# Other start addresses for TensorE's operands: moving ones at 160, stationary ones at 384 bytes modulo 512

## The chip, the cores and the metric

The kernel runs on one core of one Trainium2 chip. The metric is the device time of one execution in microseconds (us). On-chip memory (SBUF) has 128 partitions, and a tile takes the same range of byte addresses in each of them. A matmul on TensorE (PE) has two operands in SBUF. The stationary one (the weights) is brought into the array by an instruction of its own, LDWEIGHTS, which the profile lists as engine PEld. The moving one then streams through, column by column. What this document calls the residue of an operand is the byte address of its first element in a partition, modulo 512.

## The reference

Two blocks follow each other, for 8 batches of 3136 rows of 256 numbers.

```python
X = np.fft.rfft(x, axis=1)
Yr = Xr @ w_r - Xi @ w_i + b_r
Yi = Xr @ w_i + Xi @ w_r + b_i
Yr = np.sign(Yr) * np.maximum(np.abs(Yr) - 0.01, 0.0)      # the same for Yi
x = np.fft.irfft(Yr + 1j * Yi, n=3136, axis=1)

h = np.maximum(x @ w_in, 0.0)                              # 256 -> 1024
conv_out[s] = sum(conv_w[k] * h[s + k - 1] for k in 0, 1, 2)
out = (h / (1 + np.exp(-conv_out))) @ w_out                # 1024 -> 256
```

The biases are drawn and then enlarged by about 35; w_in, conv_w and w_out come as 64-bit numbers.

## The kernel before, in words

**The spectral part.** The transform of length 3136 = 56 x 56 is done as two stages of small matmuls each way. Stage 1 (line 247, its head for the first batch at line 262) multiplies rows of x by a table. Stage 2 (L282) multiplies by tables `t2`. `mix` (L306) applies w_r and w_i. Stage 3 (L333) starts the way back with the tables `i1_hi` and `i1_lo`. A work item is one batch and one of seven groups of 4 frequencies, so there are 56 items; one pass over the loop at L372 does stage 2 of item `it`, the mix of `it - 1`, stage 3 of `it - 3`, and stage 1 for a later batch. Between stages 1 and 2, and again between stages 3 and 4, data goes through DRAM.

**The feed-forward part.** Stage 4 (L421) ends the inverse transform. `up` (L440) is the product with w_in, for two pieces of 448 columns (450 with their neighbours) and one of eight slices `f` of 128 hidden features; ScalarE (ACT) and VectorE (DVE) then do the activation, the three taps and the gate (L442 to L455). `down` (L468) is the product with w_out, four slices behind, so that PE has work while a slice is being gated. There are 28 chunks of 8 slices, and a slice has 12 matmuls of `up` and 21 of `down`.

**Precision.** Where the text says hi and lo (`wmix_hi`, `yh`, `gl` and so on), a number is split into two, and three matmuls stand for one: hi by hi, hi by lo, lo by hi. These run in a format that the profile shows as f32 and the program calls float32r. Stages 1, 2 and 4 use plain float32, and each of their matmuls appears twice in the profile: 11,088 in the program are 12,096 in the trace.

**The shapes that matter here.** In mix and `down` the moving operand is 256 columns of weights (`wmix`, `wout`), which is 1024 bytes, and the stationary one 128 columns of data (`fh`, `fl`, `gh`, `gl`), 512 bytes. In stage 3 the moving operand is 256 columns of data (`sh`, `sl`), and the stationary one 112 columns of a table, 448 bytes. In `up` the moving operand is 450 columns of `yh` or `yl` and the stationary one 128 columns of `win`. All the matmuls of these four have a new stationary operand each.

**Order and addresses.** The order on each engine comes from a scheduler that simulates a time line; tiles lie one behind the other in pools. `cst` lies lowest, from address 16512 on (128 modulo 512). Its first tile is a pad of 384 bytes, so `win`, `wout` and everything in the pools behind them begin at multiples of 512; the small constants (`i2`, the tap weights, a threshold) share one tile of 1024 bytes, `cst_s`. Because `i1_hi` and `i1_lo` have 448 bytes for each frequency, the stationary operand of stage 3 is the only one of the whole program that does not start at residue 0. Its residues run through 0, 448, 384, 320 or 256, 192, 128, 64 over the four frequencies of an item, and `i1_lo` is 256 further than `i1_hi`; the moving operand there is at 0.

Of the kernel before, what the change touches and what calls it, by code (L numbers as in the profile page):

```python
# [9 lines left out]
F32 = mybir.dt.float32  # L10
# [17 lines left out]
P = 128  # L28
NT = D // P
NF = FF // P  # L30
# [65 lines left out]
def spectral_ffn_kernel(ctx: ExitStack, tc: tile.TileContext, x, w_r, w_i, b_r, b_i,  # L96
                        w_in, conv_w, w_out, fwd1, fwd2, inv1, inv2, out):
    nc = tc.nc
    K1, K2 = 2 * R, 2 * SP
# [5 lines left out]
    cst = ctx.enter_context(tc.tile_pool(name="cst", bufs=1))  # L105

    cst.tile([P, 96], F32, name="pad")
    win = [cst.tile([P, NT, FF], F32R, name=f"win_{q}") for q in range(2)]  # L110
    wout = [cst.tile([P, NF, D], F32R, name=f"wout_{q}") for q in range(2)]
    cst_s = cst.tile([P, 2 * P], F32, name="cst_s")
    i2 = cst_s[0:K1, 0:K1]
    cw = cst_s[:, P:P + 3 * NF].rearrange("p (k f) -> p k f", k=3)
    mlam, warm = cst_s[:, P + 3 * NF:P + 3 * NF + 1], cst_s[:, P + 3 * NF + 1:P + 3 * NF + 2]


    with ExitStack() as ab:
# [5 lines left out]
        cmx = ab.enter_context(tc.tile_pool(name="cmx", bufs=1))  # L124
# [5 lines left out]

        f1 = c1.tile([K1, P], F32, name="f1")[:, 0:K1]
        t2 = c1.tile([K1, U, K2], F32, name="t2")
        bias = cmx.tile([P, 2, UG // 2, D], F32, name="bias")
        wmix_hi = cmx.tile([P, NT, 3, D], F32R, name="wmix_hi")
        wmix_lo = cmx.tile([P, NT, 3, D], F32R, name="wmix_lo")
# [223 lines left out]
        with tc.issue_after(st.ins):  # L359
# [3 lines left out]
            for i in range(2):  # L363
                a2s[i], ld = load_a2(*items[i])
        ab.enter_context(tc.issue_after(ld.ins))
        wkf, wk, cab, io = [ab.enter_context(tc.tile_pool(name=nm, bufs=n, reuse_waits="tile"))
                            for nm, n in (("wkf", 2), ("wk", 2), ("cab", 1), ("io", 2))]
        i1_hi = cab.tile([K2, U, K1], F32R, name="i1_hi")
        i1_lo = cab.tile([K2, U, K1], F32R, name="i1_lo")
        background = later()  # L370
# [23 lines left out]
    def pool(name, bufs=1, **kw):  # L394
        return ctx.enter_context(tc.tile_pool(name=name, bufs=bufs, reuse_waits="tile", **kw))

    zio, y_a = pool("zio", 3), pool("y_a")
    wk, hp, io, y_b = pool("cwk"), pool("chp", 3), pool("cio"), pool("y_b")
    SW = 3168
    hp.tile([P, 8], F32, name="pad", bufs=1)  # L400
    psh, pso = pool("psh", 2, space=PSUM), pool("pso", space=PSUM)

    JG = 4
# [95 lines left out]
    for st in range(n_st + LAG):  # L499
        if st < n_st:  # L500
            ci, f = divmod(st, NF)
# [10 lines left out]
        if st >= LAG:  # L512
            ci, f = divmod(st - LAG, NF)
# [25 lines left out]
```

## Time and profile before

| | |
|---|---|
| time, median of 3 runs (lowest to highest) | 1779.51 us (1778.32 to 1780.85) |
| time of the profiled execution | 1777.15 us |
| its span, first to last instruction | 1775.4 us |
| PE / PEld busy | 1742.4 / 1635.9 us |
| DVE / ACT busy | 1532.6 / 1224.9 us |
| mean granted TensorE clock | 0.995 |

The spectral part takes about the first 560 us, the feed-forward part the rest. "Busy" of PE is not a rate, because matmuls overlap: the time from the start to the end of one is longer than the distance from its start to the next one's start. That distance, called spacing here, is what adds up to the span where PE is the bound. The chain of waits gives it directly: a piece of the chain has a length and a count of matmuls.

### The profile page before, as it was taken

To read this page: it belongs to the slowest core of one execution; us is meant where nothing else is said; L and a number is where in the kernel's file an instruction comes from. 1 tells how busy PE (TensorE), PEld (TensorE's weight loads), DVE (VectorE), ACT (ScalarE), POOL (GpSimd) and SP (SyncE) were. 2 spreads that over 40 slices of the span, in tenths; PEclk is the share of its full clock that TensorE was granted. 3 is DMA by queue.
4 is the path that set the end of the run, shared out by engine and by line. 5 is a ranking of instruction groups with operands and counts; after the bars stand their busy time and mean duration, and the time that the engine had idled before them with its cause. 6 is when DMAs were issued, how large, how long until landed. Compare 5 with 4: busy or idle time off the path is not lost.

```text
span 1775.4 us, 29407 instructions
## 1 busy us (share of the span) xinstructions
PE 1742.4 (98%) x12096; PEld 1635.9 (92%) x12096; DVE 1532.6 (86%) x1842; ACT 1224.9 (69%) x1579; POOL 133.9 (8%) x60
## 2 busy tenths in 40 slices
PE   6999999999998999999999999999999999999998
PEld 3888888888997999999999999999999999999998
DVE  2999999999996988888888888888888888888887
ACT  2666667666765777777777777777767777777666
POOL 0122222222222000000000000000000000000000
PEclk8999999999999999999999999999999999999999
DMA  9776676676544110111111111111101111100001
GB/s 268 225 246 215 190 238 206 200 226 201 170 119 146 43 32 22 32 52 52 35 50 53 42 42 53 42 42 53 42 22 42 53 43 42 42 22 22 22 22 42
DMA packets 107382, 164.63 MB, mean 93 GB/s; under 512 B 8816, under 2 KB 86000, under 8 KB 107248
## 3 DMA queue, kind: packets, MB, share of 16 engines
q1 hardware_dynamic: 107248, 162.74, 30.0%
q8 instruction: 96, 1.57, 0.4%
q14 instruction: 38, 0.31, 0.1%
HBM read 85.65 MB, written 77.07 MB: 92 GB/s over the span
## 4 chain that ended last, share of the span: by engine, by line
PE 92%; DVE 3%; DMA 2%; ACT 1%; issue 1%; ACTq 0%; SPq 0%; DVEq 0%
PE acc L468 32%; PE ps_h L440 31%; PE ps_mx L306 11%; PE ps_s L421 5%; PE ps_s L282 5%; PE ps_s L247 4%; PE ps_s L333 4%; DMA i_raw<-in_inv_dram 1%; DVE v L315 1%; DVE fl L288 0%; DMA sc<-ha 0%; DVE v L321 0%; DMA z<-sc 0%; DMA a<-sc 0%; DVE p L311 0%
## 5 line engine op out<-in xcount | busy, mean ns | idle before, releaser
L468 PE MATMUL acc<-wout,gh 128*128 128x256 f32 x3136 | 576.9, 284 | 0.0
L449 DVE SCALAR_TENSOR_TENSOR c<-h,cst_s,c 128x896 f32<-128x896 f32 x448 | 512.8, 1147 | 51.2 <-ACT c L447 50.1
L440 PE MATMUL ps_h<-yh,win 128*128 128x450 f32 x1792 | 551.2, 368 | 0.6 <-DVE yl L428 0.5
L468 PEld LDWEIGHTS acc<-wout,gh 128*128 128x128 f32 x3136 | 501.5, 191 | 6.7
L468 PE MATMUL acc<-wout,gl 128*128 128x256 f32 x1568 | 442.4, 284 | 0.0
L442 ACT ACTIVATE h<-ps_h 128x900 f32<-128x900 f32 x224 | 207.4, 926 | 265.6 <-PE ps_h L440 265.5
L440 PEld LDWEIGHTS ps_h<-yh,win 128*128 128x128 f32 x1792 | 339.6, 190 | 25.9 <-DVE yl L428 1.1
L440 PE MATMUL ps_h<-yl,win 128*128 128x450 f32 x896 | 329.1, 367 | 0.0
L468 PEld LDWEIGHTS acc<-wout,gl 128*128 128x128 f32 x1568 | 299.1, 191 | 0.2
L455 DVE TENSOR_TENSOR gl<-c,gh 128x896 fp32r<-128x896 f32 x224 | 242.9, 1088 | 57.0 <-ACT gh L454 53.3
L451 DVE TENSOR_TENSOR c<-h,c 128x896 f32<-128x896 f32 x224 | 243.3, 1087 | 48.6 <-ACT c L450 48.4
L454 ACT CAST gh<-c 128x896 fp32r<-128x896 f32 x224 | 209.9, 943 | 49.7 <-DVE c L451 49.7
L450 ACT ACTIVATE c<-c 128x896 f32<-128x896 f32 x224 | 213.4, 952 | 23.4 <-DVE c L449 20.5
L306 PE MATMUL ps_mx<-wmix_hi,fh 128*128 128x256 f32 x672 | 202.7, 302 | 0.0
L306 PE MATMUL ps_mx<-wmix_lo,fh 128*128 128x256 f32 x672 | 202.0, 301 | 0.0
L306 PE MATMUL ps_mx<-wmix_hi,fl 128*128 128x256 f32 x672 | 191.1, 286 | 1.2 <-DVE fl L290 1.0
L440 PEld LDWEIGHTS ps_h<-yl,win 128*128 128x128 f32 x896 | 169.7, 189 | 10.4
L447 ACT ACTIVATE c<-h,cst_s 128x896 f32<-128x896 f32 x168 | 175.5, 1045 | 2.5
L323 POOL TENSOR_TENSOR sl<-v,sh 128x1024 fp32r<-128x1024 f32 x56 | 133.7, 2387 | 421.0 <-PE ps_s L333 247.1
L315 DVE TENSOR_TENSOR v<-ps_mx,p 64x512 f32<-64x512 f32 x224 | 153.8, 686 | 3.3
L306 PEld LDWEIGHTS ps_mx<-wmix_lo,fh 128*128 128x128 f32 x672 | 128.6, 191 | 12.7 <-issue 12.7
L306 PEld LDWEIGHTS ps_mx<-wmix_hi,fl 128*128 128x128 f32 x672 | 128.3, 191 | 10.2 <-issue 8.2
(87 smaller groups left out, 2023.3 us busy)
## 6 DMA issues: line engine op xcount, KB each, us to landing
a<-sc SPq DMA_DIRECT2D x56, 448.0 KB, 4.9
sc<-z SPq DMA_DIRECT2D x56, 448.0 KB, 3.2
z<-sc SPq DMA_DIRECT2D x56, 448.0 KB, 3.7
xr<-in_x_dram SPq DMA_DIRECT2D x55, 448.0 KB, 4.9
out_dram<-o SPq DMA_DIRECT2D x27, 896.0 KB, 4.3
sc<-a SPq DMA_DIRECT2D x49, 448.0 KB, 5.1
sc<-ha SPq DMA_DIRECT2D x7, 448.0 KB, 6.8
win_bits<-in_moe_w_in_dram SPq DMA_DIRECT2D x4, 512.0 KB, 5.5
```

The costliest lines, as they stand in the source:

```text
L306: nc.tensor.matmul(ps[c][:, k, :], lt, rh, start=(n == 0), stop=(n == len(mm) - 1))
L315: nc.vector.tensor_tensor(v[dst, :, k, :], ps[c][src], p1[src, c], op=ALU.add)
L323: SL_ENG.tensor_tensor(sl, v, sh.bitcast(F32), op=ALU.subtract)
L440: nc.tensor.matmul(ps[:, a, 0:CH + 2], lt, rh, start=(n == 0), stop=(n == len(mm) - 1))
L442: nc.scalar.activation(h, ps[:, :, 0:CH + 2], AF.Relu)
L447: nc.scalar.mul(c, h[:, :, 0:CH], cw[:, 0, f:f + 1])
L449: nc.vector.scalar_tensor_tensor(c, h[:, :, k:k + CH], cw[:, k, f:f + 1], c, op0=ALU.mult, op1=ALU.add)
L450: nc.scalar.activation(c, c, AF.Sigmoid)
L451: nc.vector.tensor_tensor(c, h[:, :, 1:CH + 1], c, op=ALU.mult)
L454: nc.scalar.copy(gh, c)
L455: nc.vector.tensor_tensor(gl, c, gh.bitcast(F32), op=ALU.subtract)
L468: nc.tensor.matmul(acc[m // 2][:, m % 2, :], lt[:, sl], rh[:, f, :], start=(f == 0 and n == 0 and m % 2 == 0), stop=(f == NF - 1 and n == ...
```

## The change

No instruction is added, taken away or moved. Set aside line numbers and the numbers in tile names, the rows of all five engines stand in the same order before and after, 11,090 on PE among them. What changes is where tiles lie.

- `i2` and `cw` become tiles of their own and come first (448 and 96 bytes), the pad of 384 bytes goes, and `mlam` and `warm` move to a tile of 128 bytes behind `wout`. So `win` and `wout` begin at 16512 + 544 = 17056 and so on, which is 160 modulo 512.
- A pad of 384 bytes stands ahead of `bias` and `wmix`, pads of 224, 224 and 288 bytes in the pools of stage 3 and mix (`cab`, `wkf`, `wk`), and one of 96 bytes ahead of the tiles of the gate (`cwk`).

| matmul (line before) | count | moving: before, after | stationary: before, after |
|---|---|---|---|
| mix (L306) | 2016 | 0, 160 | 0, 384 |
| stage 3 (L333) | 672 | 0, 160 | all multiples of 64, the same |
| `down` (L468) | 4704 | 0, 160 | 0, 384 |
| `up` (L440), even batches | 1344 | multiples of 128; 288 plus these | 0, 160 |
| `up` (L440), odd batches | 1344 | multiples of 128, the same | 0, 160 |
| stage 4 (L421) | 448 | 0, 128 | 0, 288 |
| stage 2 (L282) | 448 | 0, 288 | 0, 288 |
| stage 1 (L247, L262) | 112 | 0; 288 (160 in the head) | 0, 288 |

The tiles that ACT, DVE, GpSimd and the DMA queues use move with them (`xr`, `a2` and `z2` to 288, `c`, `gh` and `gl` to 384, `sh`, `sl` and `v` to 160, the three buffers of `h` from 32, 64, 96 to 416, 448, 480).

```diff
     cst = ctx.enter_context(tc.tile_pool(name="cst", bufs=1))
-    cst.tile([P, 96], F32, name="pad")
+    i2 = cst.tile([K1, K1], F32, name="i2")
+    cw = cst.tile([P, 3, NF], F32, name="cw")
     win = [cst.tile([P, NT, FF], F32R, name=f"win_{q}") for q in range(2)]
     wout = [cst.tile([P, NF, D], F32R, name=f"wout_{q}") for q in range(2)]
-    cst_s = cst.tile([P, 2 * P], F32, name="cst_s")
-    i2 = cst_s[0:K1, 0:K1]
-    cw = cst_s[:, P:P + 3 * NF].rearrange("p (k f) -> p k f", k=3)
-    mlam, warm = cst_s[:, P + 3 * NF:P + 3 * NF + 1], cst_s[:, P + 3 * NF + 1:P + 3 * NF + 2]
+    small = cst.tile([P, 32], F32, name="small")
+    mlam, warm = small[:, 0:1], small[:, 1:2]
...
         t2 = c1.tile([K1, U, K2], F32, name="t2")
+        cmx.tile([P, 96], F32, name="pad")
         bias = cmx.tile([P, 2, UG // 2, D], F32, name="bias")
...
                             for nm, n in (("wkf", 2), ("wk", 2), ("cab", 1), ("io", 2))]
+        cab.tile([P, 56], F32, name="pad")
+        wkf.tile([P, 56], F32, name="pad", bufs=1)
+        wk.tile([P, 72], F32, name="pad", bufs=1)
         i1_hi = cab.tile([K2, U, K1], F32R, name="i1_hi")
...
     hp.tile([P, 8], F32, name="pad", bufs=1)
+    wk.tile([P, 24], F32, name="pad", bufs=1)
```

## The prediction

> **What bounds the kernel now.** I read first the page's busy times and the sum of the chain of waits, to see which engine sets the end; then two wide windows, to see how close the next engine is in each part; then the pieces of the chain, which give the spacing of matmuls; and last the rows of single lines with their shortest, median and longest durations.
>
> ```profile
> PE 1742.4 (98%) x12096; PEld 1635.9 (92%) x12096; DVE 1532.6 (86%) x1842; ACT 1224.9 (69%) x1579; POOL 133.9 (8%) x60
> PE 92%; DVE 3%; DMA 2%; ACT 1%; issue 1%; ACTq 0%; SPq 0%; DVEq 0%
> 50.00:540.00 490.00, 485.70 (x3626) 437.68 (x3626) 463.41 (x764) 338.04 (x538) 126.55 (x53) 1.00 0.66 201
> 640.00:1700.00 1060.00, 1060.00 (x7208) 1022.01 (x7208) 912.02 (x907) 755.45 (x881) 0.00 (x0) 1.00 0.12 39
> ```
>
> The second row is the chain: 92% of it is PE. The other two are windows (length, then PE, PEld, DVE, ACT, POOL busy, granted clock, DMA share). In the feed-forward window PE is never idle and the clock is full, so a nanosecond less in every matmul is a nanosecond less in the span. DVE is at 912/1060 = 86% there. In the spectral window it is at 463.4/490 = 94.6%, which is little room.
>
> Now the spacing. These are pieces of the chain: start, length, what, how many.
>
> ```profile
> 160.38 3.12 PE ps_mx L306 x26
> 163.50 1.41 PE ps_s L333 x12
> 165.77 1.78 PE ps_s L282 x16
> 167.55 1.19 PE ps_mx L306 x10
> 169.60 3.12 PE ps_mx L306 x26
> 1483.89 3.23 PE acc L468 x27
> 1487.12 2.46 PE ps_h L440 x12
> 1494.07 1.77 PE ps_s L421 x16
> ```
>
> Mix runs at 3.12/26 = 120.0 ns, `down` at 3.23/27 = 119.6 ns, stage 3 at 1.41/12 = 117.5 ns, all three with 256 moving columns. `up`, with 450, runs at 2.46/12 = 205 ns. Stages 2 and 4 have only 128 and 112 moving columns and still need 1.78/16 and 1.77/16 = 111 ns. What repeats at 111 ns there whatever streams is the load of 128 weight columns, so 111 ns is the least that I count on for mix and `down`. One pass of the spectral loop is 169.60 - 160.38 = 9.22 us and holds 26 + 10 = 36 matmuls of mix.
>
> So mix and `down` are about 9 ns above the floor, and it has to be asked whether addresses have a part in that. The rows of single lines answer it (count, durations in ns as minimum/median/maximum, starts, form). A duration is 163 ns longer than the spacing: 283 against 120.0.
>
> ```profile
> L468 PE MATMUL acc<-wout,gh x2774: 277/283/365, 639.8 to 1699.9; 128*128 128x256 f32 x199
> L306 PE MATMUL ps_mx<-wmix_hi,fh x638: 278/283/687, 59.8 to 539.9; 128*128 128x256 f32 x160
> L333 PE MATMUL ps_s<-sh,i_hi x212: 275/280/284, 61.3 to 537.9; 128*112 128x256 f32 x106
> L333 PE MATMUL ps_s<-sl,i_hi x212: 274/282/284, 65.2 to 538.0; 128*112 128x256 f32 x106
> ```
>
> Stage 3 is the only place where the stationary residue varies while the moving one stays at 0. One item of it, in two windows: the first frequency (stationary residues 0 and 256, with the first row of the next one), then from the middle of the third frequency on.
>
> ```profile
> L333 PE MATMUL ps_s<-sh,i_hi x2: 276/276/277, 449.2 to 449.5; 128*112 128x256 f32 x2
> L333 PE MATMUL ps_s<-sl,i_hi x1: 276/276/276, 449.3 to 449.3; 128*112 128x256 f32 x1
> L333 PE MATMUL ps_s<-sh,i_lo x1: 278/278/278, 449.4 to 449.4; 128*112 128x256 f32 x1
> L333 PE MATMUL ps_s<-sh,i_lo x2: 280/281/282, 449.7 to 450.1; 128*112 128x256 f32 x2
> L333 PE MATMUL ps_s<-sh,i_hi x2: 281/282/283, 449.9 to 450.2; 128*112 128x256 f32 x2
> L333 PE MATMUL ps_s<-sl,i_hi x2: 281/282/283, 450.0 to 450.3; 128*112 128x256 f32 x2
> ```
>
> Same line, same shapes, same moving residue, and the spacing goes from 276 - 163 = 113 ns to 283 - 163 = 120 ns with the stationary residue. So the read of the weights and the read of the moving columns get in each other's way, and where they start decides how much. That is the whole lever of this change.
>
> **The change part by part.** *`down`, 4704 matmuls.* Both operands leave residue 0 for 160 and 384, a difference of 224. No row of before has operands an odd multiple of 32 bytes apart, so the new spacing is bounded, not read. From below by 111 ns (the weight load). From above, among the rows with these lengths, by 284 - 163 = 121 ns. At 120 they sit at the upper end of the band, and their fastest rows (277, spacing 114) show that the same shapes can go quicker. I take 115 ns, between the 113 of the best residues in stage 3 and its mean of 117.5, as the nearest rows with 256 moving columns whose operands start apart. That is 5 ns x 4704 = 23.5 us; the ends are 9 ns, 42.3 us, and -1 ns, 4.7 us lost.
>
> *Mix, 2016 matmuls.* The same shapes and the same pair of residues: 5 ns x 2016 = 10.1 us (18.1 gained to 2.0 lost). Per pass that is 36 x 5 = 0.18 us of 9.22. DVE's work per pass is 0.946 x 9.22 = 8.72 us, so 9.04 is still over it, and I count it in full; the cover is 0.32 us a pass.
>
> *Stage 3, 672 matmuls.* Its stationary residues still run through all multiples of 64, the moving one goes to 160. There is no longer an item whose first frequency starts level, but none stays at one place either. I take 117.5 as before; bounds 113 and 121, 3.0 us gained to 2.4 lost.
>
> *`up`, 2688 matmuls.* In even batches moving and stationary operands are again multiples of 128 apart, only in another order. In odd batches they come to be 32 off these. The rows of before:
>
> ```profile
> L440 PE MATMUL ps_h<-yh,win x1584: 360/367/374, 641.2 to 1698.1; 128*128 128x450 f32 x198
> L440 PE MATMUL ps_h<-yl,win x792: 363/367/372, 641.5 to 1697.9; 128*128 128x450 f32 x198
> ```
>
> They spread by 7 ns either way of the median over the residues that occur. I take nothing for both halves; the bounds are 7 ns x 1344 = 9.4 us up or down, for the odd batches.
>
> *Stages 1, 2 and 4.* Stages 2 and 4 run at the weight load's 111 ns, so a moving stream that is read better or worse has to cross that first. I take nothing.
>
> *DVE, ACT and DMA.* Every tile moves for them too. `h` has three buffers at residues 32, 64 and 96, and an operation that reads it in turn from all three hardly varies:
>
> ```profile
> L451 DVE TENSOR_TENSOR c<-h,c x198: 1073/1086/1104, 641.8 to 1697.4; 128x896 f32<-128x896 f32 x198
> L442 ACT ACTIVATE h<-ps_h x198: 901/922/967, 643.9 to 1698.5; 128x900 f32<-128x900 f32 x198
> ```
>
> So I take nothing; what hides it if I am wrong is PE's lead of 14% in the feed-forward part and 5% in the spectral part. DMA is at 0.66 of its engines in the spectral window, under PE, and hides there. No wait is added and no queue is passed: the order of all engines is the same.
>
> *The sum.* 23.5 + 10.1 = 33.6 us off the profiled execution's 1777.15 gives 1743.6. The three runs' median is 2.4 us over that execution, so 1746 us is the forecast. The extreme ends of the terms are 1779.5 - 42.3 - 18.1 - 3.0 - 9.4 = 1707 and 1779.5 + 4.7 + 2.0 + 2.4 + 9.4 = 1798.
>
> The Trainium skill ("TensorE: Matmul & The Clock Gate", Part 2, step 1) says that TensorE has two independent read ports into SBUF and that loading the next weights does not take bandwidth from the running matmul. By that rule no address could matter, and the time would stay at 1779.5. The trace disagrees, with 276 against 283 ns in stage 3. The same page ("Back-to-back issue gap") gives N/2.4 + 2.5 ns for a stream without loads; an estimate from it is 109.2 ns for 256 columns, by which the two terms would be 72 us and the time 1707.
>
> **The rivals.**
>
> *DVE takes over the spectral part.* The cover is only 0.32 us a pass, and DVE itself waits for ACT now and then. If no pass gets shorter, the gain of mix is lost: 1746 + 10.1 = 1756 us. For it speaks the 94.6%; against it that DVE works ahead of PE in that loop by an item.
>
> *Nothing happens.* Mix and `down` go through hundreds of equal loads at a level 120, and a fixed rhythm of the two streams could pull itself into the same step from any start, because the next load starts with the next matmul. What the start addresses shift would then be undone in a few matmuls: 1779.5 us. For it speaks that the medians of mix and `down` are both 283 although other tiles and engines surround them. Against it speaks stage 3, where twelve matmuls in a row do not settle. The rule on two ports would give the same time by another road.
>
> *Slower: the level start was the good one.* In stage 3 the operands that start level (residues 0 and 256 against 0) are the fast ones, 276, 276 and 278 with a mean of 276.7, and those that start apart take 277 to 283, some 281.4 in the mean of the item's other rows. Mix and `down` start level now. If their 120 is the price of 16 more weight columns, and starting apart costs the same 281.4 - 276.7 = 4.7 ns again, they go to 124.7 ns: 4.7 x 6720 = 31.6 us, so 1811 us. It decides as soon as the median duration of the two lines is above 283. Against it stands that no row with 256 moving columns is over 284 outside of waits.
>
> **How the numbers follow.** The forecast (mix and `down` between 111 and 118 ns) has 0.46, and its own range is 1707 to 1766 us (118 ns: 2 x 6720 = 13.4 us off). DVE in the way of mix: 0.10. Nothing happens: 0.17. Slower: 0.27, and within it a small loss is about as likely as the full 4.7 ns. About 0.2% (3.6 us) is what a measurement of this kernel can tell from no change. So faster has 0.46 + 0.10 + 0.01 from a very small gain, 0.57; the same 0.16; slower 0.27. For the range I leave out the lowest end, where both lines would run at the weight load's floor, and the upper part of the slower case: 1718 to 1804 us.
>
> **What would show it.** In the changed profile the same pieces of the chain: `down` and mix at 115 x count, and their median durations near 278. Right in mechanism and wrong in size would be a median that has moved, but to another value than 278. The forecast is wrong if it stays at 283 or goes above. `up` is checked by its durations, 367 in even and odd batches; stage 3 by 280 to 282; stages 2 and 4 by 111 ns. The rival on DVE is seen if L306's durations fall while a pass stays near 9.2 us and PE shows idle time that DVE ends. If DVE's or ACT's durations move by more than 2%, my reading of `h`'s three buffers was wrong.

## The result, and the profile after

| | before | after |
|---|---|---|
| time, median (lowest to highest) | 1779.59 us (1778.32 to 1780.85) | 1771.45 us (1766.68 to 1798.75, 4 executions) |
| ratio of the two, 95% interval | | 0.9945 [0.9924, 0.9967] |
| span of the profiled execution | 1775.4 us | 1797.0 us |

The change makes the kernel faster by about 8 us by the medians, and by about 10 us by the ratio; the forecast was 33.5 us. The executions of the changed kernel fall into two groups at the same granted clock (0.991 to 0.993): three lie between 1766.7 and 1772.0 us, one at 1798.75; the ratio is that of the three, and the profile is of the one above, so its spectral part is not that of the median.

The page of after, busy times and the sum of its chain of waits:

```profile
PE 1745.9 (97%) x12096; PEld 1627.7 (91%) x12096; DVE 1568.6 (87%) x1842; ACT 1223.6 (68%) x1579; POOL 134.9 (8%) x60
PE 70%; DVE 15%; issue 8%; DMA 3%; ACT 3%; SPq 0%; DVEq 0%; ACTq 0%
```

DVE has 36 us more work than before with the same 1842 instructions, and 15% of the chain in place of 3%. The two wide windows of after show where (length, then PE, PEld, DVE, ACT, POOL busy with counts):

```profile
50.00:540.00 490.00, 468.08 (x3413) 411.61 (x3412) 472.21 (x718) 316.54 (x510) 118.61 (x50) 1.00 0.68 198
640.00:1700.00 1060.00, 1060.00 (x7275) 1020.70 (x7274) 920.79 (x916) 763.08 (x891) 0.00 (x0) 1.00 0.13 41
```

In the feed-forward window PE ran 7275 matmuls in the time in which it ran 7208 before, 0.9% more. In the spectral window it ran 3413 in place of 3626, and DVE took more time (472.2 against 463.4 us) for fewer instructions (718 against 764).

The spacing, from the pieces of the chain. Of before, the 104 matmuls that end the program:

```profile
1758.21 12.49 PE acc L468 x104
```

and of after:

```profile
524.98 2.84 PE ps_mx L305 x24
642.17 3.16 PE acc L471 x27
1042.42 3.90 PE ps_h L443 x19
1780.29 12.27 PE acc L471 x104
```

`down` went from 12.49/104 = 120.1 ns to 118.0 and 3.16/27 = 117.0 ns, mix from 120.0 to 2.84/24 = 118.3 ns; `up` stayed at 205. The rows of single lines of after say the same (minimum/median/maximum):

```profile
L471 PE MATMUL acc<-wout,gh x2784: 274/280/367, 642.1 to 1698.3; 128*128 128x256 f32 x199
L305 PE MATMUL ps_mx<-wmix_hi,fh x653: 276/280/686, 50.0 to 569.8; 128*128 128x256 f32 x164
L332 PE MATMUL ps_s<-sh,i_hi x212: 274/280/290, 64.4 to 566.8; 128*112 128x256 f32 x106
L443 PE MATMUL ps_h<-yh,win x1596: 361/367/375, 640.0 to 1699.8; 128*128 128x450 f32 x200
```

The medians of `down` and mix went from 283 to 280, not to 278.

What a chain's pieces give in samples, the starts of all matmuls give in full. I took the distance from the start of each matmul to the next one's start, added them up by line, and use these sums below. For mix and stage 3, "within the line" is the mean of the distances under 150 ns between two matmuls of that line, so that waits are left out:

```
                          before      after
down   4703 distances   566.0 us   555.6 us    120.35 -> 118.14 ns
up     2688             552.5      552.7       205.53 -> 205.62
mix    within the line                         119.69 -> 117.35
stage 3 within the line                        116.99 -> 117.82
```

So `down` gave 10.4 us and `up` nothing. That alone covers the whole difference of the medians, 8.1 us. Mix is 2.3 ns shorter in spacing, but its last matmul starts 569 us after the first instruction on PE, against 540 before.

**What happened in the spectral part.** VectorE in after, one piece of its time line (start, length, line, output <- inputs):

```profile
169.12 2.46 DVE L289 TENSOR_TENSOR fl<-d,fh 128x512 fp32r<-128x512 f32 x1
171.50 0.68 DVE L201 TENSOR_TENSOR win<-win_m,win_rest 128x512 fp32r<-128x512 f32 x1
172.10 2.80 DVE L314 TENSOR_TENSOR v<-ps_mx,p 64x512 f32<-64x512 f32 x4
...
179.47 2.72 DVE L289 TENSOR_TENSOR fl<-d,fh 128x512 fp32r<-128x512 f32 x1
```

and GpSimd in after, with what released it in brackets:

```profile
158.66 2.35 POOL L322 TENSOR_TENSOR sl<-v,sh 128x1024 fp32r<-128x1024 f32 x1 [6.80 <-PE ps_s L332]
168.67 2.36 POOL L322 TENSOR_TENSOR sl<-v,sh 128x1024 fp32r<-128x1024 f32 x1 [7.66 <-ACT sh L321]
179.29 2.36 POOL L322 TENSOR_TENSOR sl<-v,sh 128x1024 fp32r<-128x1024 f32 x1 [8.26 <-ACT sh L321]
```

The same two engines before, VectorE first:

```profile
163.77 0.68 DVE L290 TENSOR_TENSOR fl<-d,fh 128x512 fp32r<-128x512 f32 x1
164.37 0.68 DVE L202 TENSOR_TENSOR win<-win_m,win_rest 128x512 fp32r<-128x512 f32 x1
164.97 2.81 DVE L315 TENSOR_TENSOR v<-ps_mx,p 64x512 f32<-64x512 f32 x4
```

and GpSimd before:

```profile
164.96 2.35 POOL L323 TENSOR_TENSOR sl<-v,sh 128x1024 fp32r<-128x1024 f32 x1 [6.52 <-PE ps_s L333]
174.18 2.36 POOL L323 TENSOR_TENSOR sl<-v,sh 128x1024 fp32r<-128x1024 f32 x1 [6.87 <-PE ps_s L333]
```

The low part `sl` is the one job of GpSimd here, a subtraction of two tiles in SBUF. Its single buffer is free when stage 3 of the pass before has read it. Before, that release comes last, and `sl` runs beside `v` (L315), which reads PSUM and one tile of SBUF: neither is slowed. In this execution of after the release by ACT's `sh` comes last at 168.67, and `sl` then runs beside `fl` (L289), which reads two tiles of SBUF. At 169.12 `fl` starts 0.45 us into `sl` and takes 2.46 us in place of 0.68: it ends 0.55 us after `sl` does, as if it had only begun then. PE waits for `fl`; these are waits of after (in total us, times, longest). Before, the last two were 1.9 and 1.0 us:

```profile
POOL sl L322 <- PE ps_s L332: 240.6, 35, 8.7
POOL sl L322 <- ACT sh L321: 210.6, 21, 63.2
PEld ps_mx L305 <- DVE fl L289: 25.0, 35, 1.4
PE ps_mx L305 <- DVE fl L289: 16.6, 24, 1.2
```

### The profile page after: what moved, and what is told of

It reads as the page before. It is cut to its first block, busy times and chain, and to the rows that moved or that the text cites. A ratio compares the mean times of both kernels' runs of the same rounds, so it can differ in the third digit from the quotient of the medians.

```text
span 1797.0 us, 29407 instructions
## 1 busy us (share of the span) xinstructions
PE 1745.9 (97%) x12096; PEld 1627.7 (91%) x12096; DVE 1568.6 (87%) x1842; ACT 1223.6 (68%) x1579; POOL 134.9 (8%) x60
## 4 chain that ended last, share of the span: by engine, by line
PE 70%; DVE 15%; issue 8%; DMA 3%; ACT 3%; SPq 0%; DVEq 0%; ACTq 0%
PE acc L471 31%; PE ps_h L443 31%; PE ps_s L424 5%; DVE v L314 5%; DVE fl L287 2%; PE ps_mx L305 2%; DMA i_raw<-in_inv_dram 2%; DVE p L310 2%; ACT r L319 2%; DVE fl L289 2%; DVE d L286 1%; DVE v L320 1%; PE ps_s L332 1%; PE ps_s L281 1%; DMA z<-sc 0%
## 5 line engine op out<-in xcount | busy, mean ns | idle before, releaser
L471 PE MATMUL acc<-wout,gh 128*128 128x256 f32 x3136 | 567.0, 280 | 0.0
L452 DVE SCALAR_TENSOR_TENSOR c<-h,cw,c 128x896 f32<-128x896 f32 x448 | 512.9, 1147 | 47.1 <-ACT c L450 46.1
L471 PEld LDWEIGHTS acc<-wout,gh 128*128 128x128 f32 x3136 | 493.7, 188 | 6.5
L471 PE MATMUL acc<-wout,gl 128*128 128x256 f32 x1568 | 437.6, 281 | 0.0
L471 PEld LDWEIGHTS acc<-wout,gl 128*128 128x128 f32 x1568 | 293.6, 188 | 0.1
L454 DVE TENSOR_TENSOR c<-h,c 128x896 f32<-128x896 f32 x224 | 243.5, 1087 | 46.8 <-ACT c L453 46.6
L450 ACT ACTIVATE c<-h,cw 128x896 f32<-128x896 f32 x168 | 175.6, 1045 | 2.6 <-DVE gl L458 0.2
```

What stands on the lines that cost most here:

```text
L450: nc.scalar.mul(c, h[:, :, 0:CH], cw[:, 0, f:f + 1])
L452: nc.vector.scalar_tensor_tensor(c, h[:, :, k:k + CH], cw[:, k, f:f + 1], c, op0=ALU.mult, op1=ALU.add)
L454: nc.vector.tensor_tensor(c, h[:, :, 1:CH + 1], c, op=ALU.mult)
L471: nc.tensor.matmul(acc[m // 2][:, m % 2, :], lt[:, sl], rh[:, f, :], start=(f == 0 and n == 0 and m % 2 == 0), stop=(f == NF - 1 and n == ...
```

## The experiments

My theory after this was in two parts: the streams of weights and of columns do get in each other's way by their addresses, by less than I had taken; and the spectral loop has a good and a bad rhythm, told apart by when GpSimd starts. Rivals: the gain comes from something else that the change did (the other order of the constants, ACT's or DVE's addresses); and DVE is slowed by the new addresses of its own operands.

**e1, the price of an address.** A program of matmuls alone, with 16 moving and 16 stationary operands at all multiples of 32 bytes modulo 512 (`mv[a]` at 32 a, `sta[b]` at 32 b), each pair repeated:

```diff
...
+    for cols, n, times in ((128, 256, 24), (112, 256, 16), (128, 450, 16)):
+        for a in range(16):
+            for b in range(16):
+                for k in range(times):
...
+                        nc.tensor.matmul(ps[0:cols, 0:n], sta[b][:, 0:cols], mv[a][:, 0:n], start=True, stop=True)
...
```

> Another program altogether: nothing of the reference is computed. It runs the same matmul over and over, with nothing else on the chip: for each of 16 x 16 pairs of moving and stationary residue (0, 32, ... 480) 24 times with 128 weight columns and 256 moving ones, 16 times with 112 and 256, 16 times with 128 and 450. Theory (residues set the spacing): 120 ns at moving 0 and stationary 0, 117 to 119 at 160 and 384 with 128 and 256 columns, other pairs from 113 to 121; the best pair under 116. Rival (a common rhythm pulls every pair into the same step): all 256 pairs within 1 ns of 120, and the 118 of the changed kernel would come from the rest of the program.

Rows of the map's lines L46 (128 weight columns, 256 moving) and L48 (112 weight columns); the letters a, b, c, d, i stand for residues 0, 32, 64, 96 and 256:

```profile
L46 PE MATMUL acc<-ma,sb x24: 276/280/285, 8.8 to 11.5; 128*128 128x256 f32 x24
L46 PE MATMUL acc<-ma,sc x24: 276/276/282, 11.6 to 14.2; 128*128 128x256 f32 x24
L46 PE MATMUL acc<-ma,sd x24: 282/283/285, 14.3 to 17.1; 128*128 128x256 f32 x24
L46 PE MATMUL acc<-mi,sa x24: 277/283/284, 369.6 to 372.3; 128*128 128x256 f32 x24
L48 PE MATMUL acc<-ma,sa x16: 278/279/281, 733.2 to 735.0; 128*112 128x256 f32 x16
L48 PE MATMUL acc<-ma,sc x16: 281/283/284, 737.0 to 738.8; 128*112 128x256 f32 x16
```

Mean spacing from the ninth matmul of each pair on, by stationary minus moving address modulo 256, 0 being called level (of the 32 pairs of each column the mean; level at 128 weight columns without the very first pair, whose first 17 distances after the program's start are near 213 ns):

```
difference        0      32     64     96     128    160    192    224
128 w, 256 mv   120.0  118.5  117.1  117.8  118.7  120.1  117.8  117.7 ns
112 w, 256 mv   117.8  117.4  119.8  117.5  118.4  117.7  119.7  118.0
128 w, 450 mv   203.2  205.4  206.7  206.6  204.1  207.0  200.0  203.5
```

In most pairs only the difference matters. The sign is the one of the theory, and the size is smaller: all eight columns of the first row lie within 3 ns, where I had taken 5 for this one difference. The pair of the change, 224, is at 117.7 ns, 2.3 below level. Some differences have two values, and which one a pair takes was not foreseen: 64 bytes gives 113.3 ns in five pairs (the row `ma,sc` is one) and 117.7 to 117.9 in the other 27; 96 gives 117.3 in 25 pairs, 118.7 in two and 120.0 in five (`ma,sd` is one). Level is among the worst with 128 weight columns and not with 112: stage 3, from which I had read the size, follows another line of this table than `down`.

**e2, `down` alone.** The kernel before, with pads that move the operands of `down`. Two other things move with them, though the expectation says otherwise: `i2`, the moving operand of stage 4, comes to 160 and so 96 bytes off its stationary one, and the tiles of the gate change places with those of `h`:

```diff
     win = [cst.tile([P, NT, FF], F32R, name=f"win_{q}") for q in range(2)]
+    cst.tile([P, 40], F32, name="pad_w")
     wout = [cst.tile([P, NF, D], F32R, name=f"wout_{q}") for q in range(2)]
...
-    wk, hp, io, y_b = pool("cwk"), pool("chp", 3), pool("cio"), pool("y_b")
+    hp, wk, io, y_b = pool("chp", 3), pool("cwk"), pool("cio"), pool("y_b")
...
+    wk.tile([P, 64], F32, name="pad", bufs=1)
```

> The kernel before with only the operands of the down-projection at 160 and 384; mix, stage 3 and up keep theirs (the odd batches of up start 256 bytes further, which leaves their difference to the weights a multiple of 128). Theory (the gain of the change is all in the down-projection, 120.3 - 118.2 = 2.1 ns times 4704 = 9.9 us): 1769 to 1771 us, ratio 0.9945, and the spectral part as before, 9.22 us a pass. Rival (mix shares the gain by its count): 70% of the 8 us, 1774 us.

1766.15 us (1764.98 to 1766.99), ratio 0.9931 [0.992, 0.9943]. Its feed-forward window:

```profile
640.00:1700.00 1060.00, 1060.00 (x7277) 1021.11 (x7275) 921.26 (x917) 764.23 (x893) 0.00 (x0) 1.00 0.13 40
```

7277 matmuls, as in after (7275). `down`'s distances add up to 554.0 us at 117.81 ns, 12.0 us below before, and the time fell by 11.9, 3 us more than I had expected. Stage 4 takes 101.2 us in place of 99.6, so the gain is not from there. The addresses of `down` account for all of the gain; the order of the constants and the rest of the change are not needed. That the difference of the addresses does it, and not the pads, is what e9 settles.

**e3, mix and stage 3 alone.** (14 matmuls of stage 1's head move too.)

```diff
         t2 = c1.tile([K1, U, K2], F32, name="t2")
+        cmx.tile([P, 40], F32, name="pad")
...
+        cab.tile([P, 56], F32, name="pad")
+        wkf.tile([P, 56], F32, name="pad", bufs=1)
+        wk.tile([P, 72], F32, name="pad", bufs=1)
```

> The kernel before with only the operands of mix and stage 3 at the residues of the change; down-projection and up are untouched. Theory (a faster mix shifts GpSimd's subtraction onto VectorE's instructions with two SBUF inputs, which then wait for it): no gain, 1778 to 1800 us, and in the profile the subtraction for the third of the three sums (fl from d and fh) at 0.9 us or more instead of 0.70, passes over 9.22 us. Rival (mix gains 2 ns as the down-projection does, and the profile of the changed kernel was only a disturbed run): 2 ns times 2016 = 4 us, 1775 to 1776 us, VectorE's durations as before.

Two groups again, at the same granted clock (0.991 to 0.994 and 0.993 to 0.995): seven executions from 1775.43 to 1778.05 us, seven from 1803.60 to 1805.64. The ratio of the lower group is 0.9989 [0.9979, 0.9999]. A stretch of the spectral loop before, and the group of instructions in question (busy time, mean ns):

```profile
200.00:300.00 100.00, 100.00 (x739) 89.11 (x738) 94.79 (x152) 70.49 (x112) 25.97 (x11) 1.00 0.69 217
L290 DVE TENSOR_TENSOR fl<-d,fh 128x512 fp32r<-128x512 f32 x53 | 37.2, 702 | 0.1
```

and in e3, whose profile is of the upper group:

```profile
200.00:300.00 100.00, 95.79 (x694) 83.88 (x695) 98.03 (x143) 65.32 (x106) 23.68 (x10) 1.00 0.63 194
L291 DVE TENSOR_TENSOR fl<-d,fh 128x512 fp32r<-128x512 f32 x49 | 46.9, 957 | 0.1
```

694 matmuls in 100 us in place of 739: a pass takes 9.22 x 739/694 = 9.82 us, with VectorE at 98%. Mix's spacing is 117.01 ns all the same. The bad rhythm belongs to the spectral part and costs 27 us; the lower group gives 2 us, although mix is 2.7 ns quicker. No profile of e3's lower group was caught, so that it runs in the good rhythm is concluded from its time.

`fl` is not the only one that grows. I compared every instruction of VectorE in the first 600 us that overlaps `sl` with the median of the same instruction where it does not. Added up, they take longer by 12.6 us before, 41.4 in after and 41.1 in e3; `fl` has 1.0, 13.8 and 13.6 of these. The largest others come from the conversion of w_in and w_out that runs beside the spectral loop (`win`, `wout`, `win_e`, `wout_e`). From before to e3 that is 28.5 us more, and the time is 27 us longer.

**e4, `sl` held back.** After, with a copy of one number on GpSimd ahead of `sl`, which reads the last element that `fl` writes, so that `sl` can't start ahead of `fl`'s end:

```diff
...
+            if behind is not None:
+                SL_ENG.tensor_copy(small[0:1, 2:3], behind[0:1, NT - 1, 2, UG - 1, SP - 1:SP].bitcast(F32))
             SL_ENG.tensor_tensor(sl, v, sh.bitcast(F32), op=ALU.subtract)
...
```

> The changed kernel, with GpSimd's subtraction held back until VectorE has finished the subtraction that follows stage 2 of the next item: a copy of one number from that result on GpSimd ahead of it. Theory (the two block each other): the mean of that subtraction on VectorE falls from 0.96 to 0.70 us, a pass takes 9.15 us, and the time is 1779.6 - 9.9 - 4 = 1766 us or a little under, with runs that agree within 0.3%. Rival (the long durations are a state of the chip in that execution): the runs lie between 1766 and 1799 us as the changed kernel's, with the long durations in some.

Seven executions from 1768.01 to 1771.26 us, five from 1786.40 to 1790.74; median 1770.67, ratio to before over all twelve 0.9995 [0.9964, 1.0027]. (The median of before beside it is 1778.07; the seven lower ones lie 7 to 10 us under it.) The profile is of the lower group:

```profile
200.00:300.00 100.00, 100.00 (x746) 89.10 (x745) 95.20 (x154) 70.12 (x112) 27.67 (x22) 1.00 0.71 210
L289 DVE TENSOR_TENSOR fl<-d,fh 128x512 fp32r<-128x512 f32 x53 | 36.3, 686 | 0.1
```

In it `fl` is at 686 ns, and the loop runs 746 matmuls in 100 us, 1% more than before: here mix's shorter spacing does reach the pace of the loop. It does not reach the end: mix's last matmul starts at 541.2 us, against 539.9 before. From 100 to 540 us e4 ran 3329 matmuls and before 3294, but from 50 to 100 us 315 against 334; what the start-up lost there was not tried. The end of mix in e7, below, is much the same, 540.5 us. The upper group lies at 1786 to 1791 us with the hold, and at 1799 in the one such execution of after. The hold does not remove it, and no profile of that group was caught: it was not a sufficient cure, and what is left of it stays open.

**e7, GpSimd reads nothing.** As e3, with a memset in place of the subtraction:

```diff
-            SL_ENG.tensor_tensor(sl, v, sh.bitcast(F32), op=ALU.subtract)
+            SL_ENG.memset(sl.bitcast(F32), 0.0)
```

> The kernel with only mix and stage 3 at the new residues, and GpSimd filling the low part of the thresholded spectrum with zeros instead of subtracting: it reads nothing then, and the low part is left out of the result. Theory (VectorE's instructions with two SBUF inputs wait for GpSimd's reads): the long durations vanish, the subtraction from d and fh takes 0.68 us each time, all runs lie in one group, at 1774 to 1777 us. Rival (the slow group is a state of the chip or comes from the addresses that VectorE reads): two groups as before, 1776 and 1804 us.

1774.30 us, all eleven executions from 1771.69 to 1778.61, ratio 0.9977 [0.9965, 0.9989]. `fl` and GpSimd's job in e7:

```profile
L291 DVE TENSOR_TENSOR fl<-d,fh 128x512 fp32r<-128x512 f32 x54 | 36.9, 683 | 0.7 <-ACT fh L290 0.4
L324 POOL MEMSET sl<- 128x1024 f32 x53 | 50.5, 952 | 453.8 <-PE ps_s L334 453.8
```

The upper group is gone, with the addresses of e3. In seven places `fl` and the memset overlap, and `fl` has a mean of 681 ns there; in e3 it overlaps the subtraction in 17 places, with a mean of 1480 ns and a longest of 2742. All of VectorE's instructions together are 0.4 us longer beside the memset. The memset is also shorter (0.95 against 2.39 us), so this run doesn't part the reading from the length as causes of the rhythm; for the slowing of a single `fl` it does, since an overlap with a write costs nothing. The Trainium skill ("SBUF — State Buffer", Who interferes with whom) says that a VectorE instruction with two SBUF inputs contends with a GpSimd instruction that reads SBUF and not with one that only writes it, and that the ports which the two share are an exclusive lock. The traces agree: 1480 against 681 ns.

With VectorE's wait taken away, mix and stage 3 at the new addresses are worth 4 us here (0.0023 x 1778.3). Where they show is not seen in the profiled execution, which at 1777.5 us is one of the longest of the eleven.

**e8, the rhythm without the addresses.** Mix, `down`, `up` and stage 3 with the differences of before, but two buffers for `sl`, so that stage 3 no longer holds GpSimd back. The constants also have the order of after, and the tiles of the spectral part lie 192 bytes further modulo 512:

```diff
...
-            sl = wk.tile([K2, UG, D], F32R, name="sl", bufs=1)
+            sl = wk.tile([K2, UG, D], F32R, name="sl")
...
```

> The kernel before with all operands of each matmul as far apart as they were, and two buffers instead of one for the low part of the thresholded spectrum, so that GpSimd no longer waits for stage 3 and starts as soon as ScalarE has rounded the high part. Theory (when GpSimd starts decides, not the addresses): it falls on VectorE's subtraction from d and fh, which takes 0.9 us or more in the mean, and all runs are at 1795 to 1806 us. Rival (the new addresses of mix make the slow group): 1778 us and 0.70 us.

1799.22 us, all four from 1798.36 to 1800.03, ratio 1.0113 [1.01, 1.0127]. Groups and a window of e8:

```profile
L289 DVE TENSOR_TENSOR fl<-d,fh 128x512 fp32r<-128x512 f32 x50 | 47.8, 956 | 0.1
L322 POOL TENSOR_TENSOR sl<-v,sh 128x1024 fp32r<-128x1024 f32 x51 | 121.8, 2389 | 416.8 <-ACT sh L321 405.5 <-PE ps_s L332 11.3
200.00:300.00 100.00, 98.45 (x716) 86.72 (x714) 98.03 (x150) 66.60 (x108) 26.14 (x11) 1.00 0.66 196
```

`fl` has 956 ns, as in e3, with no operand of mix off level (its spacing is 119.66 ns). So the new addresses of the matmuls are not needed for the loss; and in e7 VectorE's operands lie as in e3, where it was slowed, and it is not. The time at which GpSimd starts decides, and the wait for one buffer was what kept it in a harmless place. What makes one execution of e3 fall into the one group and the next into the other was not found.

**e5 and e6, the map used.** The spectral part level, as before. In e5 `down` has a difference of 224 and `up` 192, the best of the map's third row. e6 is e5 with `down` at 64:

```diff
-    cst.tile([P, 96], F32, name="pad")
+    i2 = cst.tile([K1, K1], F32, name="i2")
+    cw = cst.tile([P, 3, NF], F32, name="cw")
...
-    SW = 3168
-    hp.tile([P, 8], F32, name="pad", bufs=1)
+    SW = 3200
+    zio.tile([P, 8], F32, name="pad", bufs=1)
+    wk.tile([P, 40], F32, name="pad", bufs=1)      # e6: hp in place of wk
```

> The kernel before with mix and stage 3 as they were (operands level), the down-projection 224 bytes apart modulo 256 as in the change, and up with weights 192 bytes past the moving operand modulo 256 for both rows of y and both buffers (rows of y 128 bytes longer each). Theory (only the difference modulo 256 counts, as the map of pairs has it: 200.0 ns at 192 for 450 columns, where the kernel before has a mean of 205.3): the down-projection's 12 us and 5 ns x 2688 = 13.4 us off, 1753 us. Rival (up's three matmuls a row alternate operands and rows, so that the even rhythm of the map does not come about): no more than the down-projection's share, 1766 us.

> As the run before in this list, but the down-projection's operands 64 bytes apart modulo 256. In the map that difference has two steady spacings, 113.3 ns in some pairs and 117.8 in most. Theory (the pair starts in the one or the other by the phase of what ran before): a mean between the two, 115 to 117.5 ns, so 1 to 13 us under the run before. Rival (after up's matmuls it always falls into the common one): 117.8, the same time as the run before within 3 us.

e5: 1764.13 us (1762.31 to 1764.66), ratio 0.9914 [0.9901, 0.9928]. e6: 1763.75 us (1761.33 to 1765.48), ratio 0.9913 [0.9898, 0.9928]. Rows of e5:

```profile
L468 PE MATMUL acc<-wout,gh x2825: 277/280/367, 640.1 to 1699.1; 128*128 128x256 f32 x189
L440 PE MATMUL ps_h<-yh,win x1611: 361/363/370, 642.4 to 1699.9; 128*128 128x450 f32 x179
```

and of e6:

```profile
L468 PE MATMUL acc<-wout,gh x2820: 276/276/367, 640.0 to 1697.8; 128*128 128x256 f32 x188
L440 PE MATMUL ps_h<-yh,win x1615: 361/369/374, 641.1 to 1699.9; 128*128 128x450 f32 x180
```

In e5 `up` falls to 363 (mean spacing 203.37 ns, 5.8 us in all), not to the map's 200.0; in e6 `down` falls to 276 (116.24 ns, 19.3 us below before; the median distance is 114), near the fast one of the two values at 64, and `up` goes back to 369 (205.26 ns), though none of its operands lies elsewhere than in e5. So e6 is not under e5: `down` gave 6.1 us more and `up` 5.1 us less. Both beat after and before, but by less than the two sums, which fall by 19.0 us in e5 and 20.1 in e6, while the time falls by 14.2 and 14.6. Stage 4 takes 3 us more than before in both, and mix ends 3.5 us later; why, was not tried.

**e9 and e10, slow places of the map.** e6 with `gh` and `gl` moved so that `down`'s difference is 160, the worst of the map, and 96:

```diff
-    hp.tile([P, 40], F32, name="pad", bufs=1)
+    wk.tile([P, 24], F32, name="pad", bufs=1)      # e10: 8
+    hp.tile([P, 16], F32, name="pad", bufs=1)      # e10: 32
```

> As the kernel e6_up64, but the stationary operands of the down-projection lie 160 bytes above its moving ones modulo 256 instead of 64; nothing else is at another address. Theory (the spacing follows the difference of the two addresses modulo 256, as the map of e1 has it): 160 is as bad as level, 120.1 ns, so the 4704 matmuls go from e6's 116.2 ns back to about 120, 18 us more: 1780 to 1782 us, with the pads and the other order of the constants all still there. Rival (any place off level does, or the gain comes from another part of the change, such as the constants' order): the time stays at 1764 to 1768 us and the spacing at 116 to 118. The up-projection's operands are where they were in e5 and e6, where its spacing was 203.1 and 205.2 ns: either of the two is taken as possible, 5 us apart.

> As e6_up64, but the down-projection's difference is 96 bytes modulo 256. Theory: the map of e1 has 117.3 to 117.8 ns for 96 at 128-row weights and 256 columns, so about 117.5 in place of e6's 116.2: 6 us more than e6 for the down-projection, 1768 to 1770 us if the up-projection stays at 205.2 ns, 1763 to 1765 if it goes to the 203.1 of e5. Rival (any place off level does): as e6, 1763.8 us.

e9: 1775.66 us (1772.45 to 1777.58; a tenth execution at 2865.55, with a granted clock of 0.556, is left out), ratio 0.9989 [0.9979, 0.9999]. e10: 1773.63 us (1768.90 to 1777.40), ratio 0.9975 [0.9964, 0.9986]. Rows of e9:

```profile
L469 PE MATMUL acc<-wout,gh x2792: 277/281/366, 639.8 to 1699.0; 128*128 128x256 f32 x200
L441 PE MATMUL ps_h<-yh,win x1595: 360/363/373, 641.0 to 1699.8; 128*128 128x450 f32 x200
```

The sums of the four kernels with the same `up` addresses and pads of the same total:

```
        difference   down              up                 time
e6          64     116.24 ns 546.7 us  205.26 ns 551.7 us  1763.75 us
e5         224     117.53    552.8     203.37    546.6     1764.13
e10         96     119.30    561.1     204.30    549.2     1773.63
e9         160     120.70    567.7     202.18    543.5     1775.66
```

From e6 to e9 the sums of `down` and `up` change by about 21 - 8 = 13 us, and the time by 11.9. e5 and e9 differ only in where the gate's tiles lie, which puts `down`'s difference at 224 or 160. At 160 `down` is as slow as level, with every pad and the other order of the constants in place: the rival that any place off level does has fallen. At 96 I expected 117.5 and got 119.3; the map has 117.3, 118.7 and 120.0 at that difference, and I had read the 120.0 as one exception. And `up` takes anything from 202.2 to 205.3 ns with its operands at the same addresses; it is quickest where `down` is slowest and slowest where `down` is quickest. Why was not found, and it stays open.

## Why the prediction was right or wrong

**The lever was real.** That the spacing follows how far apart the two operands start is what e5 and e9 show: the same kernel with pads of the same size is 14.2 us under before at a difference of 224 and 1.9 us under it at 160. What in the chip makes it so, no run here shows. The rival "nothing happens" has fallen with it, as has the rival "the level start was the good one" for 128 weight columns (120.0 ns level, the second worst of eight). For the 112 of stage 3 it holds in part: level is 117.8 there, 64 and 192 apart 119.8 and 119.7. The Trainium skill's rule ("TensorE: Matmul & The Clock Gate", Part 2, step 1), that loading the next weights takes no read bandwidth from the running matmul, would have left the spacing as it was. The runs disagree with that outcome: 120.35 ns for `down` before and 117.81 in e2.

**The terms of `down` and mix were mis-sized: this is the step that failed.** The forecast was 33.5 us and the medians differ by 8.1; of the 25.4 us between them 13.1 are `down`'s, and most of the rest is mix's 10.1. By the prediction's own sign, a median that moved, but to 280 and not to 278, the mechanism was right and the size wrong. For `down`: "I take 115 ns, between the 113 of the best residues in stage 3 and its mean of 117.5", 23.5 us. Measured: 118.14 ns in after and 117.81 in e2, so 10.4 and 12.0 us.

The fault was the row from which the size came. The 276 of stage 3 was read as the price of residues 0 and 256; the map has 279 for residue 0 in steady running (`ma,sa` of L48), with 113.3 ns in two pairs of another difference only. Nor could those rows tell an address from a place in the run: over all 56 items before, the medians of the distance after the first, second and fourth of the twelve matmuls of an item are 113 ns, and after the others 115 to 121, while each place always has the same difference modulo 256. The fourth already starts at another difference (192), and the map has 119.7 for that one. In after the same places have 117 to 118 ns. So 113 ns is what the first matmuls after another line had at these addresses, and not what the addresses cost in a long run. The mean of the same line, 117.5, was the better witness, and with it the term would have been 4704 x 2.5 = 11.8 us. That it comes so near is partly luck, since it is a mean over four differences with 112 weight columns, which the map has at 117.8 to 119.8.

**The term of mix was counted in full, and nearly nothing arrived.** The spacing fell by 2.3 to 2.7 ns (5 us of the 10.1 by size), and in the good rhythm the loop runs 1% quicker (746 against 739 matmuls in 100 us). But e3 gives 2 us in its lower group and loses 27 in its upper one, so of the 10.1 us at best 2 arrived (4 in e7, where GpSimd reads nothing). The "cover of 0.32 us a pass" under which I left VectorE was right as arithmetic and missed that VectorE's own work is not fixed: one `fl` grows by up to 2.1 us (0.68 to 2.74) when GpSimd's job falls beside it, and all of VectorE's instructions together by 41 us.

**The rival on DVE**, at a chance of 0.10 and a price of 10 us, named the engine that takes mix's gain in the upper group. It foresaw the signs: the durations of mix fall, and PE waits for `fl`. It did not foresee the loss, because it took VectorE's instructions as they were. e8 shows that loss with mix level as before. In the lower group of e4, where `fl` is not slowed, mix's gain doesn't reach the end either, and that is not explained.

**What was taken at nothing.** Stage 3 went from 116.99 to 117.82 ns, 0.6 us lost, inside its bounds. `up` did not move in after (205.53 and 205.62 ns), but e5 and e9 show that it can, by 6 and 9 us. Stage 4 and its waits add up to 102.8 us in after, 99.6 before, and 102 to 104 in e5 to e10, whether its operands lie as before (e7, 102.7) or not; a cause was not looked for. "If DVE's durations move by more than 2%, my reading of `h`'s three buffers was wrong": those of `fl` moved (702 to 957 ns), in another place and for another reason, so that sentence tested the wrong thing. The operations that read `h` kept their means in the feed-forward part: 1147 ns (L449 before) and 1087 (L451) before and after. That reading was right.

## What to carry to other kernels

Before a size is read from the fastest rows of a line, look whether the mean of that line says the same: the first matmuls after a change of line can have another spacing than a long run at the same addresses. A gain in an engine that another follows at 95% is to be worked out with the instructions that may grow when the order in time shifts, above all VectorE's with two SBUF inputs beside a GpSimd job that reads SBUF. And a wait for a single buffer can be what keeps two engines apart: taking it away cost 1.1% here (e8).

## What the runs showed of the hardware that was not expected

- The spacing of float32r matmuls with a weight load each follows, in most pairs of e1, the difference of their operands' addresses modulo 256: the means lie between 117.1 and 120.1 ns for 128 weight and 256 moving columns and between 200.0 and 207.0 ns for 450. The pattern is another one with 112 weight columns.
- Some differences have two values of spacing in different pairs, with nothing else running (64 bytes: 113.3 ns in five pairs, 117.7 to 117.9 in 27). In e5, e6, e9 and e10 `up` takes 202.2 to 205.3 ns with its operands at the same addresses, when only `down`'s move.
- The executions of one kernel can fall into two groups 27 us apart (e3, seven and seven) at the same granted clock.
- A 0.68 us instruction of VectorE took up to 2.74 us beside a 2.36 us job of GpSimd that reads SBUF, and 0.68 beside one that only writes.
